# A third stacked-v buffer, a wider gate on the third pair's inputs, and another order of steps in a kernel that chains a gated recurrence into a cosine MLP

## The chip, the cores and the metric

The kernel runs on one core of a Trainium2 chip. The metric is the device time of one execution in microseconds (us). Before the change three runs took 188.55, 185.67 and 186.45 us, a median of 186.45.

## What is computed

The reference is a recurrence over 768 tokens for 4 batches and 8 heads of width 48, and an MLP with the gate h·cos(h) over the 3072 tokens that come out of it:

```python
for t in range(S):
    state = alpha[:, :, t, :, None] * state + np.einsum('bhd,bhe->bhde', k[:, :, t], v[:, :, t])
    y[:, :, t] = np.einsum('bhd,bhde->bhe', q[:, :, t], state)
...
h = x @ w_in            # 384 -> 2048
g = h * np.cos(h)
return (g @ w_out)      # 2048 -> 384
```

All inputs and the output are float32.

## The kernel before

**Tiling.** The tokens of a batch are cut into 3 pieces of 256, so there are 12 pieces J = 0 to 11, which the change calls pairs (each is a pair of chunks c = 0, 1 of 128 tokens; inside a chunk even and odd tokens, e = 0, 1, lie in separate halves). "The third pair" is J = 2, "the fourth" J = 3. Each pair passes the same steps. I write a step as name(J, ...):

- load(J, a/k/q/v): one 384 KB DMA each, issued from SP (L107 to 121). w1(u) and w2(u): a quarter of w_in or w_out each, cast to bf16 on the way, issued from POOL (L125 to 135).
- mula(J) on POOL and ln(J) on ACT make the logarithms of alpha; cums0, cums on PE sum them (L173 to 195); sub, icp, exps (together "eb" for later pairs, L223) make the exponentials; sk(J, e) and sq(J, e) scale k and q with them on POOL or, with ":D", on DVE (L231 to 237); castv(J) on POOL makes the bf16 v (L239).
- trans (PE, L281) and evT (L291) give k and q transposed; scores (PE, L297) and mask (DVE, L306) give the masked products; outer (PE, L313), add (DVE, L330) and state (POOL, L340) carry the state on.
- **Stacked v.** yT needs v with its halves rearranged, in one of NS tiles "vs" (L85), used in turn: vs_t[J % NS]. For J = 0 to 2 this is done by vpe on PE and vev on ACT or DVE (L251 to 261); for later pairs by vst, four SBUF-to-SBUF DMAs of 64 KB from SP (L242 to 247). A vst or vev for pair J must wait until yT(J - NS) has read the tile.
- yT (PE, L347) makes the recurrence's output, evy (L375) copies it as the MLP's input xT.
- m1(J, u) (PE, L385): a quarter of the first matmul, 12 instructions; sin(J, u) on ACT (L393), gate(J, u) on DVE (L398); m2(J, c, part) (PE, L408): 4 instructions; evo copies the result (L422), out writes it (L434, from SP).

The outputs of cums0, vpe, trans, scores, outer, yT and m1 share three PSUM buffers of one tag ("h", two banks each). A step that takes one waits until the last reader of the tile that was there is done.

**What sets the order.** Nothing is scheduled by the compiler. The table PLAN gives every step a number; all steps are issued in the order of these numbers, and each engine (PE, ACT, DVE, POOL, and SP for DMAs) works through its own in that order. An engine that must wait holds everything behind it. IDLE places matmuls on zeros in PE's order, whose results nobody reads.

**A gate.** GATES says that load(2, a) carries a semaphore wait on the last matmul of yT(1). As SP works in order, all loads that come after it in the PLAN wait too.

```python
NL, NQ, NV, NS = 4, 3, 3, 2
...
GATES, AFTER = {("a", 2): ("yT", 1)}, {}
```

Of the kernel before, what the change touches and what calls it, by code (L numbers as in the profile page):

```python
# [16 lines left out]
def kernel(  # L17
# [10 lines left out]
    nc = tc.nc  # L28
    B, H, S, D = q.shape
    DM, DF = moe_w_in.shape  # L30
    C = 128
# [9 lines left out]
    NU = NF // FW  # L41
    MP = 4

    NL, NQ, NV, NS = 4, 3, 3, 2
    BUF = {"a": 4, "in": 3, "cp": 3, "qkT": 3, "A": 2, "un": 4, "us": 2, "c": 3, "xT": 3, "g": 4}

    consts = ctx.enter_context(tc.tile_pool(name="consts", bufs=1))
# [48 lines left out]

    a_sb, kqv, cp_sb, icp_sb, qkT_sb, A_sb, c2_sb = {}, {}, {}, {}, {}, {}, {}
    xT, gsb = {}, {}
    GATES, AFTER = {("a", 2): ("yT", 1)}, {}
    src = {"a": alpha, "k": k, "q": q, "v": v}  # L100

    def pass_gate(step, last):
# [1 line left out]
            if gate == step:  # L104
                AFTER[key] = last

    def load(nm, J):  # L107
        b, g = J // NJB, J % NJB
        t = sb.tile([C, H, 2, D], FP, tag=nm, name=nm, bufs=BUF["a" if nm == "a" else "in"])
        dma = nc.sync.dma_start(  # L110
            out=t.rearrange("p h e d -> p h (e d)"),
            in_=src[nm][b, :, g * T2 : (g + 1) * T2, :].rearrange("h (p e) d -> p h (e d)", e=2),
        )
        if (nm, J) in AFTER:
            tc.add_manual_dep(dma.ins, AFTER[nm, J].ins.name,
                              mybir.DependencyInfo(mybir.DependencyClass.Sync, mybir.DependencyReason.DATA),
                              reason="inputs of later pairs stay behind the weights")
        if nm == "a":
            a_sb[J] = t
        else:  # L120
            kqv[nm, J] = t
# [261 lines left out]
    h_ps, c_sb, o_ps, o_sb = {}, {}, {}, {}  # L383

    def mlp1(J, u):  # L385
        h_ps[J, u] = ps.tile([C, FW, T2], FP, tag="h", name="h_ps", bufs=3)
        for f in range(FW):
            ft = u * FW + f
            for kk in range(KT):
                nc.tensor.matmul(h_ps[J, u][:, f, :], w1[:, kk, ft * C : (ft + 1) * C], xT[J][:, kk, :],  # L390
                                 start=(kk == 0), stop=(kk == KT - 1))

    def cosine(J, u):  # L393
        act_set("trig")
# [13 lines left out]
    def mlp2(J, c, part):  # L408
# [7 lines left out]
        fts = range(part * NF // MP, (part + 1) * NF // MP)  # L416
        for o, cols in zip(o_ps[J, c], HALVES if last_tile else [slice(0, DM)]):
            for ft in fts:
                nc.tensor.matmul(o[:, 0 : cols.stop - cols.start], gsb[J][:, ft, c * C : (c + 1) * C], w2[:, ft, cols],  # L419
                                 start=(done == 1 and ft == fts[0]), stop=(done == MP and ft == fts[-1]))  # L420

    def evict_o(J, c, copy):  # L422
        if (J, c) == (NJ - 1, 1):
# [17 lines left out]
    def idle(n):  # L441
# [3 lines left out]
            nc.tensor.matmul(idle_ps[0], zeros[:, 0:C], zeros, start=True, stop=True)  # L445

    copies = {"DVE": nc.vector.tensor_copy, "ACT": nc.scalar.copy}
    mults = {"DVE": nc.vector, "POOL": nc.gpsimd}
    steps = {
        "load": lambda J, nm: load(nm, J), "w1": load_w1, "w2": load_w2,  # L450
        "mula": mul_a, "ln": ln, "cums0": cums0, "cums": cums, "sub": sub, "icp": icp, "exps": exps, "eb": session,
        "sk": lambda J, e, eng="POOL": scale_k(J, e, mults[eng]), "sq": lambda J, e, eng="POOL": scale_q(J, e, mults[eng]),
        "castv": cast_v, "vst": stack_v, "vpe": stack_v_pe,
# [6 lines left out]


    PLAN = {
# [64 lines left out]
    }  # L527
    IDLE = [(45, 10), (155, 2), (345, 9), (375, 1), (435, 4), (485, 3)]

    order = []  # L530
    for key, line in PLAN.items():
# [42 lines left out]
```

## Time and profile before

| | |
|---|---|
| median of three runs | 186.45 us (185.67 to 188.55) |
| the profiled execution | 185.78 us, of which the span from first to last instruction is 184.0 us |
| busy: PE, DVE, ACT, POOL | 173.0, 134.5, 124.9, 83.5 us |
| first m1 begins | 17.32 us |
| yT(1) begins | 24.28 us |
| first m2 begins | 32.40 us |
| trans(2) begins | 41.26 us |
| last matmul group begins | 179.35 us |

How to read it: the profile is of one execution. Engines' busy times overlap, so the share of PE (94%) says how little of the span it stands still, not how much of its peak it reaches. A DMA's time "to landing" counts from its issue to the moment when its data may be used. A row of the timeline or of the chain of waits gives start, duration, engine, source line, what it writes and reads, and how many instructions were merged; in brackets is the idle time before it and what ended it.

### The profile page before, as it was taken

The numbers are of one execution on the slowest core, as the hardware profiler recorded it, in microseconds if no ns is written. First come the engines' busy times: TensorE is split into PE (matmuls) and PEld (weight loads), VectorE is DVE, ScalarE is ACT, GpSimd is POOL, SyncE is SP. The second block draws the span as 40 slices with busy tenths as digits, with TensorE's granted clock in tenths as the row PEclk, the third lists the DMA queues.
The fourth block names the chain that finished last, engine by engine and source line by source line (L and its number), as shares of the span: only waits on it lengthen the run. The fifth ranks groups of instructions, "written<-read, shape, count | busy, mean of one in ns | idle before, by whom it ended". The sixth has DMA issues, their size and how long they took to land.

```text
span 184.0 us, 5742 instructions
## 1 busy us (share of the span) xinstructions
PE 173.0 (94%) x2457; PEld 125.5 (68%) x2458; DVE 134.5 (73%) x182; ACT 124.9 (68%) x157; POOL 83.5 (45%) x116
## 2 busy tenths in 40 slices
PE   7989579979999999999999999999899999999993
PEld 2445458646687776876787777876687677776672
DVE  7069777669999899799969898879587674734520
ACT  3745457789879999895978989869774517435201
POOL 5388550079883484939686093903901110000000
PEclk9999999999999999999999999999999999999999
DMA  6999999999999979963996579003420121010312
GB/s 146 261 248 224 216 202 206 262 256 257 261 213 262 304 170 278 260 164 85 278 289 154 140 215 245 18 6 88 143 71 4 41 88 51 0 43 4 127 44 86
DMA packets 60137, 29.47 MB, mean 160 GB/s; under 512 B 51024, under 2 KB 60112, under 8 KB 60112
## 3 DMA queue, kind: packets, MB, share of 16 engines
q1 hardware_dynamic: 56256, 25.86, 57.9%
q0 software_dynamic: 3712, 3.15, 10.6%
q8 instruction: 19, 0.31, 0.8%
q10 hardware_dynamic: 144, 0.10, 0.2%
q14 instruction: 6, 0.05, 0.1%
HBM read 25.17 MB, written 4.72 MB: 162 GB/s over the span
## 4 chain that ended last, share of the span: by engine, by line
PE 68%; DMA 11%; issue 7%; SPq 6%; POOL 5%; ACT 1%; DVE 1%; POOLq 0%; DVEq 0%
PE h_ps L390 28%; PE o_ps L419 26%; DMA v<-in_v_dram 6%; SPq L110 4%; PE y_ps L370 4%; DMA k<-in_k_dram 4%; PE A_ps L303 2%; PE T_ps L288 2%; PE U_ps L321 2%; SPq L246 2%; PE o_last L419 1%; DMA vs<-vp 1%; POOL un L343 1%; POOL a L154 1%; PE cums L168 1%
## 5 line engine op out<-in xcount | busy, mean ns | idle before, releaser
L401 DVE TENSOR_TENSOR gsb<-h_ps,c_sb 128x1024 bf16<-128x1024 f32 x48 | 58.4, 1222 | 20.0 <-ACT c_sb L396 18.8
L396 ACT ACTIVATE c_sb<-h_ps,halfpi 128x1024 bf16<-128x1024 f32 x48 | 53.4, 1114 | 28.5 <-PE h_ps L390 28.4
L390 PE MATMUL h_ps<-xT,w 128*128 128x256 bf16 x576 | 67.5, 273 | 0.7 <-DMA w<-in_moe_w_in_dram 0.5
L419 PE MATMUL o_ps<-w,gsb 128*128 128x384 bf16 x368 | 66.7, 326 | 0.0
L390 PEld LDWEIGHTS <-w 128*128 128x128 bf16 x576 | 55.4, 98 | 9.7 <-DMA w<-in_moe_w_in_dram 0.8
L419 PEld LDWEIGHTS <-gsb 128*128 128x128 bf16 x400 | 37.0, 98 | 20.8
L343 POOL TENSOR_TENSOR un<-us,c 128x384 bf16<-128x384 f32 x20 | 16.7, 836 | 33.1 <-DVE us L335 26.0
L309 DVE TENSOR_TENSOR A_sb<-A_ps,msk 128x1024 bf16<-128x1024 f32 x24 | 29.1, 1220 | 3.6 <-PE A_ps L303 3.4
L233 POOL TENSOR_TENSOR kh<-k,icp 128x384 bf16<-128x384 f32 x19 | 19.5, 1032 | 10.2 <-ACT lna L146 5.3
L237 POOL TENSOR_TENSOR qh<-q,cp 128x384 bf16<-128x384 f32 x19 | 18.8, 999 | 6.1 <-ACT cp L219 4.2
L154 POOL TENSOR_TENSOR a<-a 128x384 f32<-128x384 f32 x9 | 9.0, 997 | 11.8 <-DMA a<-in_alpha_dram 11.8
L240 POOL CAST vp<-v 128x768 bf16<-128x768 f32 x12 | 10.1, 853 | 6.4 <-DMA v<-in_v_dram 6.0
L146 ACT ACTIVATE lna<-a 128x768 bf16<-128x768 f32 x12 | 10.1, 842 | 4.1 <-DMA a<-in_alpha_dram 2.4
L141 ACT ACT_TABLE_LOAD x9 | 11.5, 1283 | 0.9 <-PEq L558 0.7
L294 DVE COPY qkT<-T_ps 128x1024 bf16<-128x1024 bf16 x17 | 11.4, 682 | 0.8 <-PE T_ps L288 0.8
L396 ACT ACT_TABLE_LOAD x9 | 11.5, 1283 | 0.2
L431 ACT COPY o_sb<-o_ps 128x384 f32<-128x384 f32 x10 | 4.8, 478 | 9.6 <-PE o_ps L419 9.6
L431 DVE COPY o_sb<-o_ps 128x384 f32<-128x384 f32 x13 | 7.2, 554 | 4.3 <-PE o_ps L419 4.2
L445 PE MATMUL idle_ps<-zeros 128*128 128x512 bf16 x28 | 9.0, 469 | 1.2 <-DVE halfpi L77 1.2
L379 DVE CAST xT<-y_ps 128x384 bf16<-128x384 f32 x14 | 7.7, 584 | 3.1 <-PE y_ps L370 2.9
L335 DVE TENSOR_TENSOR us<-U_ps,un 128x384 f32<-128x384 f32 x16 | 8.8, 551 | 1.3 <-PE U_ps L321 1.2
L303 PE MATMUL A_ps<-qkT 48*128 48x128 bf16 x192 | 8.7, 217 | 0.6 <-DVE qkT L294 0.5
(68 smaller groups left out, 149.2 us busy)
## 6 DMA issues: line engine op xcount, KB each, us to landing
a<-in_alpha_dram SPq DMA_DIRECT2D x12, 384.0 KB, 6.0
v<-in_v_dram SPq DMA_DIRECT2D x12, 384.0 KB, 6.1
k<-in_k_dram SPq DMA_DIRECT2D x12, 384.0 KB, 6.0
q<-in_q_dram SPq DMA_DIRECT2D x12, 384.0 KB, 6.2
out_dram<-o_sb SPq DMA_DIRECT2D x23, 192.0 KB, 2.3
vs<-vp SPq DMA_DIRECT2D x36, 64.0 KB, 2.8
w<-in_moe_w_in_dram POOLq DMA_DIRECT2D x4, 384.0 KB, 8.7
w<-in_moe_w_out_dram POOLq DMA_DIRECT2D x4, 384.0 KB, 10.7
```

Of the source, the lines that this page charges most:

```text
L141: nc.scalar.preload_act_table_set("natural_log_exp_and_others")
L233: eng.tensor_tensor(out=kh_t[J % NQ][:, e, :, 0:D], in0=kqv["k", J][:, :, e], in1=icp_, op=ALU.mult)
L237: eng.tensor_tensor(out=qh_t[J % NQ][:, e, :, 0:D], in0=kqv["q", J][:, :, e], in1=cp, op=ALU.mult)
L294: ins = copy(out=qkT_sb[J][:, c], in_=T_ps[J][:, c].rearrange("r n e s -> r n (e s)"))
L303: last = nc.tensor.matmul(A_ps[J, c][:, a, p, :], qkT[r, c, NP + p, :], qkT[r, c, p, :], start=True, stop=True)
L309: nc.vector.tensor_tensor(out=A_sb[J][:, c].rearrange("s a p t -> s (a p) t"), in0=A_ps.pop((J, c)).rearrange("s a p t -> s (a p) t"), in1 ...
L343: nc.gpsimd.tensor_tensor(out=u, in0=U_sum.pop(n), in1=c2_sb[J][:, :, c].unsqueeze(3).to_broadcast([C, NP, 2, D]), op=ALU.mult)
L390: nc.tensor.matmul(h_ps[J, u][:, f, :], w1[:, kk, ft * C : (ft + 1) * C], xT[J][:, kk, :], start=(kk == 0), stop=(kk == KT - 1))
L396: nc.scalar.activation(out=c_sb[J, u], in_=h_ps[J, u], func=AF.Sin, bias=halfpi, scale=1.0)
L401: nc.vector.tensor_tensor(out=gsb[J][:, u * FW : (u + 1) * FW], in0=h_ps.pop((J, u)), in1=c_sb.pop((J, u)), op=ALU.mult)
L419: nc.tensor.matmul(o[:, 0 : cols.stop - cols.start], gsb[J][:, ft, c * C : (c + 1) * C], w2[:, ft, cols], start=(done == 1 and ft == fts[0 ...
L431: copy(out=t, in_=o_ps.pop((J, c))[0][:, 0:DM])
```

## The change

- NS becomes 3: three tiles vs, so vst(J) and vev(J) wait for yT(J - 3). One more memset on POOL at the start.
- GATES also holds back k, q and v of pair 2 until yT(1). (Before, q of pair 2 was among the first nine loads.)
- load(3, a) stands among the first nine loads and has no gate.
- PLAN and IDLE are other numbers throughout: 31 idle matmuls instead of 28.
- load takes its queue as an argument, which is SP wherever the PLAN names none, and it names none. mlp1 and mlp2 report their last matmul to pass_gate; no gate refers to them.

```diff
-    NL, NQ, NV, NS = 4, 3, 3, 2
+    NL, NQ, NV, NS = 4, 3, 3, 3
...
-    GATES, AFTER = {("a", 2): ("yT", 1)}, {}
+    GATES, AFTER = {("a", 2): ("yT", 1), ("k", 2): ("yT", 1), ("q", 2): ("yT", 1), ("v", 2): ("yT", 1)}, {}
...
-    def load(nm, J):
+    def load(nm, J, queue):
...
-        dma = nc.sync.dma_start(
+        dma = queue.dma_start(
...
-        "load a": "10 20 960 1030 1170 1450 1460 2230 2570 2290 3490 2960",
-        "load k": "70 190 1040 1270 1530 2020 1990 3050 3500 4180 3440 4290",
-        "load q": "100 230 300 1290 1620 1950 2580 2850 3980 4010 3970 4770",
-        "load v": "40 290 1130 1220 1730 1930 1940 3090 3680 2990 4970 4850",
-        "w1": "330 200 470 460 - - - - - - - -",
-        "w2": "260 580 820 690 - - - - - - - -",
+        "load a": "10 100 830 610 1260 1620 1880 2240 2590 2480 3600 3710",
+        "load k": "130 430 1110 1400 1810 2210 2270 2950 3370 2990 3790 4380",
+        "load q": "220 450 870 1430 1820 2000 1980 3210 3540 4160 4510 5270",
+        "load v": "50 400 1140 1500 2140 2920 2260 3690 3570 3810 4860 5240",
+        "w1": "240 210 270 250 - - - - - - - -",
+        "w2": "790 640 860 1070 - - - - - - - -",
...
-        "castv": "90 610 1210 1260 2120 2750 2720 3760 3730 4980 5000 5360",
-        "vst": "- - - 1820 2320 3120 3110 4040 4450 5160 5010 5380",
+        "castv": "110 410 1290 1660 2150 3160 2670 3940 3590 4750 5090 5520",
+        "vst": "- - - 1930 2350 3260 3100 3950 4700 4770 5640 5720",
...
-        "yT": "490 780 1750 2150 2790 3570 3620 4330 4870 5170 5670 5970",
+        "yT": "500 820 1700 2180 2760 3510 3580 4260 4810 5110 5760 5730",
...
-    IDLE = [(45, 10), (155, 2), (345, 9), (375, 1), (435, 4), (485, 3)]
+    IDLE = [(25, 10), (145, 8), (185, 1), (325, 3), (355, 3), (415, 1), (495, 1), (575, 3), (625, 1)]
```

What the numbers mean for the first part of each queue, read from the two PLANs:

```
SP before    a0 a1 v0 k0 q0 k1 q1 v1 q2 | a2 a3 k2 v2 a4 v3 k3 q3 ...
SP after     a0 v0 a1 k0 q0 v1 k1 q1 a3 | a2 q2 k2 v2 a4 k3 q3 out(0,0) v3 ...      (| = the gate on yT(1))
POOL before  castv0 decay0 w1(1) sk(0,1) w2(0) sk(1,1) sk(1,0) w1(0) state(0,0) w1(3) w1(2) w2(1) castv1
             state(0,1) w2(3) decay1 state(1,0) w2(2) state(1,1) mula3 ...
POOL after   castv0 sk(0,0) w1(1) w1(0) w1(3) w1(2) decay0 state(0,0) castv1 sk(1,0) sk(1,1) sq(1,0) decay1
             w2(1) state(0,1) state(1,0) state(1,1) w2(0) w2(2) mula3 w2(3) ...
PE before    ... trans0 outer0 scores0 scores0 vpe0 yT0 trans1 m1(0,1) scores1 vpe1 scores1 outer1 m1(0,0) yT1
             m1(0,3) m1(0,2) m1(1,1) m1(1,2) m1(1,0) m2(0,0,1) m1(1,3) m2(0,0,3) m2(0,0,0) m2(0,0,2) cums02 ...
PE after     ... outer0 trans0 scores0 vpe1 scores0 yT0 trans1 scores1 outer1 scores1 m1(0,1) m1(0,0) m1(0,3) yT1
             m1(0,2) m1(1,1) m1(1,2) m1(1,0) m2(0,0,2) m2(0,0,0) m1(1,3) m2(0,0,1) cums02 m2(0,0,3) ...
```

DVE after, in the same stretch: sk(0,1), add(0,0), vev0, sq(0,1), sq(0,0), evT(0,1), add(0,1), mask(0,1), mask(0,0), sq(1,1), evT(1,1), mask(1,1), add(1,0), mask(1,0), add(1,1), gate(0,1), gate(0,0), gate(0,3). ACT after: evT(0,0), evy(0,0), evy(0,1), evT(1,0), vev1, sin(0,1), sin(0,0), sin(0,3), evy(1,0), evy(1,1), sin(0,2).

More of the change, by code (lines that the diff above doesn't have):

```diff
@@ L389, in mlp1 @@
             for kk in range(KT):
-                nc.tensor.matmul(h_ps[J, u][:, f, :], w1[:, kk, ft * C : (ft + 1) * C], xT[J][:, kk, :],
+                last = nc.tensor.matmul(h_ps[J, u][:, f, :], w1[:, kk, ft * C : (ft + 1) * C], xT[J][:, kk, :],
                                  start=(kk == 0), stop=(kk == KT - 1))
+        pass_gate(("m1", J, u), last)
     def cosine(J, u):
@@ L418, in mlp2 @@
             for ft in fts:
-                nc.tensor.matmul(o[:, 0 : cols.stop - cols.start], gsb[J][:, ft, c * C : (c + 1) * C], w2[:, ft, cols],
+                last = nc.tensor.matmul(o[:, 0 : cols.stop - cols.start], gsb[J][:, ft, c * C : (c + 1) * C], w2[:, ft, cols],
                                  start=(done == 1 and ft == fts[0]), stop=(done == MP and ft == fts[-1]))
+        pass_gate(("m2", J, c, part), last)
     def evict_o(J, c, copy):
@@ L447 @@
     copies = {"DVE": nc.vector.tensor_copy, "ACT": nc.scalar.copy}
+    queues = {"SP": nc.sync, "POOL": nc.gpsimd}
     mults = {"DVE": nc.vector, "POOL": nc.gpsimd}
     steps = {
-        "load": lambda J, nm: load(nm, J), "w1": load_w1, "w2": load_w2,
+        "load": lambda J, nm, eng="SP": load(nm, J, queues[eng]), "w1": load_w1, "w2": load_w2,
         "mula": mul_a, "ln": ln, "cums0": cums0, "cums": cums, "sub": sub, "icp": icp, "exps": exps, "eb": session,
```

110 rows, old and new, of the table PLAN are left out of this document.

## The prediction

> **What bounds the kernel now.** I read the page first, then busy time by stretches, then PE's waits, then the timelines of SP, POOL and PE with each early DMA's time to landing.
>
> ```profile
> span 184.0 us, 5742 instructions
> PE 173.0 (94%) x2457; PEld 125.5 (68%) x2458; DVE 134.5 (73%) x182; ACT 124.9 (68%) x157; POOL 83.5 (45%) x116
> ...
> DMA  6999999999999979963996579003420121010312
> ```
> ```profile
> 17.30:25.20 7.90, 5.34 (x117) 4.12 (x118) 6.10 (x8) 4.21 (x4) 5.30 (x8) 1.00 1.22 215
> ...
> 41.26:58.90 17.64, 17.35 (x319) 12.66 (x319) 16.63 (x22) 15.32 (x21) 14.38 (x17) 1.00 1.11 248
> 58.90:124.00 65.10, 65.08 (x1074) 49.44 (x1068) 56.49 (x69) 55.83 (x72) 39.59 (x49) 1.00 0.76 187
> 124.00:131.00 7.00, 6.20 (x105) 4.10 (x99) 5.36 (x8) 6.88 (x9) 3.94 (x6) 1.00 0.45 115
> 131.00:181.00 50.00, 49.84 (x548) 37.12 (x545) 28.70 (x31) 21.96 (x25) 5.01 (x6) 1.00 0.15 49
> ```
> The first two numbers of a stretch are its length and PE's busy time. From 41.26 us on PE stands still for 0.29 + 0.02 + 0.80 + 0.16 = 1.27 us in all. So a new order can gain almost nothing there except the 0.80, and can lose anything; the rest of what can move lies ahead of 41.26. The 0.80 is one wait, for stacked v:
>
> ```profile
> PE y_ps L370 <- DMA vs<-vp: 0.8, 1, 0.8
> ```
> The early DMAs, first their issues on SP, then on POOL, then the landings of q(1) and v(1) (issued 7.21 and 8.70), q(2) (10.18), w1(1) (8.55), w2(1) (17.18), w2(2) (23.93):
>
> ```profile
> 7.21 1.45 SPq L110 DMA_DIRECT2D q<-in_q_dram  x1
> 8.70 1.44 SPq L110 DMA_DIRECT2D v<-in_v_dram  x1
> 10.18 1.40 SPq L110 DMA_DIRECT2D q<-in_q_dram  x1
> ...
> 122.99 5.70 SPq L246 DMA_DIRECT2D vs<-vp  x8
> ```
> ```profile
> 8.55 0.93 POOL L126 DMA_DIRECT2D w<-in_moe_w_in_dram  x1
> ...
> 17.18 0.78 POOL L132 DMA_DIRECT2D w<-in_moe_w_out_dram  x1
> ...
> 23.93 0.81 POOL L132 DMA_DIRECT2D w<-in_moe_w_out_dram  x1
> ```
> ```profile
> q<-in_q_dram SPq DMA_DIRECT2D x1, 384.0 KB, 6.2
> ...
> v<-in_v_dram SPq DMA_DIRECT2D x1, 384.0 KB, 10.9
> ...
> q<-in_q_dram SPq DMA_DIRECT2D x1, 384.0 KB, 16.3
> ...
> w<-in_moe_w_in_dram POOLq DMA_DIRECT2D x1, 384.0 KB, 6.7
> ...
> w<-in_moe_w_out_dram POOLq DMA_DIRECT2D x1, 384.0 KB, 11.9
> ...
> w<-in_moe_w_out_dram POOLq DMA_DIRECT2D x1, 384.0 KB, 10.9
> ```
> So q(1) landed at 13.4, v(1) at 19.6, q(2) at 26.5: 1.45 us a load while SP's queue is alone (its issue pace), 6.2 and 6.9 once weights run beside it. w1(1) landed at 15.25 and w2(2), the last of eight, at 34.8: (34.8 - 15.25) / 7 = 2.8 us a weight.
>
> **The change, part by part.** Before, v(1) was the eighth load and the late one; k(1) and q(1) were early. After, the slots hold v(0) second (earlier by a slot), v(1) sixth, k(1) seventh, q(1) eighth. What decides when q(1) lands is when the weights begin. POOL now issues w1 behind sk(0,0), which waits for k(0):
>
> ```profile
> 9.03 0.56 DVE L233 TENSOR_TENSOR kh<-k,icp 128x384 bf16<-128x384 f32 x1 [4.49 <-DMA k<-in_k_dram]
> ```
> k(0) keeps its slot (fourth), so sk(0,0) runs from 9.0 to 10.0 (1.0 us like sq below) and w1(1) is issued at 10.0, 1.45 later than before. Before, the weights caught the eighth load; 1.45 later is one load's transfer, so I let q(1) land at 14.9 and only alpha(3) be caught. Bounds: 14.9, and 19.6 (the eighth slot's landing before); I take the low end because the shift is a whole slot.
>
> Then queues, by these durations (mean ns of one after the comma) and PE pieces:
>
> ```profile
> L401 DVE TENSOR_TENSOR gsb<-h_ps,c_sb 128x1024 bf16<-128x1024 f32 x48 | 58.4, 1222 | 20.0 <-ACT c_sb L396 18.8
> ...
> L396 ACT ACTIVATE c_sb<-h_ps,halfpi 128x1024 bf16<-128x1024 f32 x48 | 53.4, 1114 | 28.5 <-PE h_ps L390 28.4
> ...
> L309 DVE TENSOR_TENSOR A_sb<-A_ps,msk 128x1024 bf16<-128x1024 f32 x24 | 29.1, 1220 | 3.6 <-PE A_ps L303 3.4
> ...
> L237 POOL TENSOR_TENSOR qh<-q,cp 128x384 bf16<-128x384 f32 x19 | 18.8, 999 | 6.1 <-ACT cp L219 4.2 <-DMA q<-in_q_dram 1.3 <-ACT qkT L294 0.5
> ...
> L343 POOL TENSOR_TENSOR un<-us,c 128x384 bf16<-128x384 f32 x20 | 16.7, 836 | 33.1 <-DVE us L335 26.0 <-DVE us L337 7.0
> ...
> L240 POOL CAST vp<-v 128x768 bf16<-128x768 f32 x12 | 10.1, 853 | 6.4 <-DMA v<-in_v_dram 6.0 <-issue 0.4
> ...
> L335 DVE TENSOR_TENSOR us<-U_ps,un 128x384 f32<-128x384 f32 x16 | 8.8, 551 | 1.3 <-PE U_ps L321 1.2
> ...
> L294 ACT COPY qkT<-T_ps 128x1024 bf16<-128x1024 bf16 x7 | 7.0, 1010 | 1.9 <-PE T_ps L288 1.8
> ...
> L379 ACT CAST xT<-y_ps 128x384 bf16<-128x384 f32 x10 | 5.7, 597 | 3.7 <-PE y_ps L370 3.6
> ...
> L260 ACT CAST vs<-vs_ps 128x768 bf16<-128x768 f32 x3 | 2.4, 806 | 2.9 <-PE vs_ps L256 2.9
> ```
> ```profile
> 60.95 1.31 PE h_ps L390 x12
> 62.26 0.65 PE o_ps L419 x4
> ...
> 72.68 0.90 PE y_ps L370 x56
> ```
> 1. POOL: four weight issues of about 0.83 to 13.35, decay0 and state(0,0) to 14.4, castv1 to 15.3, sk(1,0), sk(1,1), sq(1,0) to 18.3. Pair 1's trans ends at about 18.95, set by POOL and by yT0 ahead of it (mask(0,0) ends on DVE at 17.45), not by q(1).
> 2. ACT: evy0 twice from 18.4 (1.2), evT(1,0) to 20.55, vev1 to 21.35. The last scores of pair 1 needs vev1's PSUM buffer: 21.4 to 21.75. All of pair 1's attention now stands ahead of the first m1, so m1(0,1) begins at 21.75, against 17.32 before; but then w1 has landed and m1 can follow m1.
> 3. DVE: mask(1,1) to 21.35, add to 21.95, mask(1,0) to 23.15, add(1,1) to 23.7. m1(0,0) waits for that second mask's buffer: 23.2. m1(0,3) 24.5 to 25.8, yT1 to 26.7. m1(0,2) waits for gate(0,0): 27.0. m1(1,1), m1(1,2) follow; m1(1,0) waits for gate(0,2), 30.9 to 32.2, where m2 begins if its weights are there.
> 4. w2(2), which m2(0,0,2) needs first, is issued behind state(1,1), which waits for add(1,1): 24.6 for state's end, w2(0) to 25.4, w2(2) from 25.4. A weight takes 2.8 beside inputs and, since a load's 1.45 is about a fifth of the 6.9 it takes beside weights, some 2.2 alone (an estimate). The five weights ahead land from 10.0 + 6.7 = 16.7 on, two or three of them beside alpha(3) (caught until 14.9 + 6.9 = 21.8), the rest alone: through at about 26.5, and the DMA runs empty. w2(0) lands at 24.6 + 6.7 = 31.3, as a first weight did, w2(2) 2.2 later, at 33.5: m2 waits 1.3. Ends: no wait, and the 11.9 of the longest landing after 25.4, 37.3; the short queue is nearest to the 6.7.
> 5. From 33.5: three m2 and m1(1,3), 3.3, then three more m2, 1.95, and the short cums: PE is at trans(2) somewhat after 38.8. trans(2) also needs k(2) and q(2). Their gate opens at 26.7 instead of 25.24 (yT1's end, first row below), but alpha(3) no longer stands in between. alpha(2) lands while the weights pause; q(2) runs beside them until w2(3) is in, near 36.5, k(2) 1.45 later, at 38. sq(2,0) and sk(2,0), 1.0 each on POOL, behind the exponentials that start at about 38, end at 40 to 40.5; I take 40.5.
>
> ```profile
> 24.61 0.63 PE L370 MATMUL y_ps<-A_sb,vs 128*32 128x128 bf16 x32
> ...
> 41.26 0.57 PE L288 MATMUL T_ps<-ident_bf,kh 64*128 64x64 bf16 x16
> ```
> trans(2) begins at 40.5 against 41.26, but two m2 groups (1.30) are still owed: 41.8, **0.55 later**.
>
> 6. **Third vs buffer.** Before, eight vst DMAs (5.70) started at 122.99, right behind yT(8), which freed the buffer; after, vst(9) waits for yT(6) and its castv stands long ahead of yT(9): **0.80 gone**. What is late next: vst(11) behind castv(11), whose way from outer(10) is add 0.55, state 0.84, castv 0.85, half of the 5.70 and the landing below, 2.8: 7.9 us. PE has two m1 and six m2 groups in between, 6.5, and seven pieces of attention, each shorter than the 0.90 of a yT; at a third of a us each 8.8 in all. No wait, by about one us.
>
> ```profile
> vs<-vp SPq DMA_DIRECT2D x36, 64.0 KB, 2.8
> ...
> L445 PE MATMUL idle_ps<-zeros 128*128 128x512 bf16 x28 | 9.0, 469 | 1.2 <-DVE halfpi L77 1.2
> ```
> 7. **The rest.** vst and out in SP's order hold the loads behind them, but I find each released several us of PE work ahead of its user. yT(6) needs add(6,1) and mask(6,0) behind three other DVE steps: some 0.3 of wait. I add **0.3** (ends 0 and, with DVE or POOL behind, 4). The three more idle matmuls stand where PE waits for ACT, POOL or DVE anyway; without that cover they cost 0.47 each. POOL makes the extra memset while it waits for v(0).
>
> Sum against the profiled execution: 185.78 + 0.55 - 0.80 + 0.3 = 185.8. The median of the runs stands 0.67 above that execution, so 186.5: no change.
>
> **Rivals.** *The weights are in time.* The DMA is empty after 26.5, so w2(0) need not take 6.7. Without the wait of 1.3: 186.5 - 1.3 = 185.2, and 184.9 without the 0.3. Against it: no weight landed sooner than 6.7 before. The Trainium skill ("DMA: Bandwidth & Descriptors", Anatomy of one DMA) has a fit for such DMAs of about 2 us plus the bytes over 436 GB/s; for 768 KB read that is an estimate of 3.8 us, by which w2(2) would be there by about 30 and this rival's time, 185.2, would come. The trace's 6.7 speaks against the rule while queues are shared.
>
> *The weights are late: slower.* Place: m2(0,0,2). w2(2) takes the 10.9 or 11.9 of before and lands at 36.3 to 37.3: 2.8 to 3.8 more, 189.3 to 190.3. From a landing of 11.8 us after issue on it is over 2%. For it: those two rows, and pair 2's loads start right beside it. Against: those two had four weights queued ahead, this one has one or none.
>
> *The weights catch q(1).* It lands at about 18.5, sq(1,0) ends at 19.5, all of steps 2 to 4 move by about 1.0: 187.5.
>
> *The third buffer does nothing*, because castv(9) or SP is late instead: 0.8 back, 187.3; the row of eight vst behind yT(8) speaks against it.
>
> **How the numbers follow.** A measurement of this kernel can tell about 2% (182.7 to 190.2) from no change. My forecast (186.5, with the dead third buffer as its upper edge) has 0.42, weights in time 0.14, q(1) caught 0.11, weights late 0.18, of which 0.10 over 190.2; waits in the long dense run that no row shows, worth 4 us or more, 0.07; a start faster by over 3.7 us, for which nothing speaks but my bounds, 0.08. Faster 0.08, slower 0.10 + 0.07 = 0.17, within 0.75. The range runs from 184.3 (the weights-in-time case less 0.6 of error) to 190.3.
>
> **What would show it.** m1(0,1) near 21.8, yT1 near 26, m2 near 33.5 after a wait for w_out; a dip of the DMA row between 25 and 30 us; trans(2) near 40.5; no wait for vs near yT(9); PE idle under 1 us after 41. Wrong it is made by a first m2 after 36, by q(1) landing after 18, or by waits of PE for masks, evictions or inputs after 45.

## The result, and the profile after the change

The changed kernel takes 186.40 us (median of 20 runs, 185.64 to 187.26), the kernel before 185.74 (20 runs taken beside them). Four of those 20, near 188 us, ran in a slower state of the chip and are left out of the ratio; one of the three runs known at the time of the prediction was such a run, which lifted their median to 186.45. The ratio is 1.0039, with a 95% interval of 1.0026 to 1.0052: slower by 0.7 us, far inside the 2% that the prediction calls no change.

The page of the changed kernel. Its span is 0.6 us longer. In the sixth of the 40 slices (23 to 28 us) the DMA engines moved 133 GB/s, where they had moved 202. The first row of GB/s is that of the changed kernel, the second that of the kernel before.

```profile
span 184.6 us, 5734 instructions
...
GB/s 146 261 261 210 204 133 202 252 246 288 236 162 268 264 169 294 227 158 119 241 281 235 204 186 4 0 97 139 169 86 91 73 44 89 0 14 32 127 87 85
```
```profile
GB/s 146 261 248 224 216 202 206 262 256 257 261 213 262 304 170 278 260 164 85 278 289 154 140 215 245 18 6 88 143 71 4 41 88 51 0 43 4 127 44 86
```

Busy time by the stretches shown before (length, then PE's busy time; the last figures are DMA share and GB/s):

```profile
32.40:41.26 8.86, 7.18 (x58) 4.52 (x56) 4.95 (x7) 7.04 (x10) 2.12 (x2) 1.00 1.14 247
41.26:58.90 17.64, 17.22 (x275) 12.57 (x276) 16.09 (x21) 15.19 (x22) 13.23 (x16) 1.00 0.99 238
58.90:124.00 65.10, 65.06 (x1069) 49.23 (x1067) 56.54 (x69) 56.56 (x74) 40.61 (x50) 1.00 0.76 179
124.00:131.00 7.00, 7.00 (x140) 5.22 (x137) 5.68 (x8) 5.57 (x8) 2.61 (x4) 1.00 0.64 164
131.00:181.00 50.00, 50.00 (x557) 37.02 (x550) 27.30 (x28) 23.11 (x27) 7.30 (x9) 1.00 0.21 66
```
The 0.80 us that PE stood still between 124 and 131 is gone, and 0.16 more behind it. What is new is in the start. PE's timeline there:

```profile
21.97 4.38 PE L390 MATMUL h_ps<-xT,w 128*128 128x256 bf16 x36 [0.30 <-DVE A_sb L309]
26.28 0.52 PE L370 MATMUL y_ps<-qkT,un 128*32 128x128 bf16 x24
...
33.28 1.46 PE L420 MATMUL o_ps<-w,gsb 128*128 128x384 bf16 x8 [0.36 <-DMA w<-in_moe_w_out_dram]
...
37.62 0.32 PE L168 MATMUL cums_h<-lna,tri 128*128 128x384 bf16 x1 [0.91 <-ACT lna L146]
...
41.55 0.41 PE L288 MATMUL T_ps<-ident_bf,kh 64*128 64x64 bf16 x16 [0.69 <-POOL kh L233]
```
trans(2) begins at 41.55 against 41.26, with two m2 groups (1.30) still owed: 1.59 us later by equal work. Less 0.80 and 0.16 that is 0.63. The last matmul group begins at 179.97 against 179.35, 0.62 later.

The logarithms of alpha(2), which cums needs, are late because ACT waits for that load. ACT's row of ln(2) and ln(3):

```profile
36.72 1.57 ACT L146 ACTIVATE lna<-a 128x768 bf16<-128x768 f32 x2 [1.35 <-DMA a<-in_alpha_dram]
```

### The profile page after: what moved, and what is told of

Its sections match the earlier page's. It is cut to its first block, busy times and chain, and to the rows that moved or that the text cites. A ratio compares the mean times of both kernels' runs of the same rounds, so it can differ in the third digit from the quotient of the medians.

```text
span 184.6 us, 5734 instructions
## 1 busy us (share of the span) xinstructions
PE 173.7 (94%) x2460; PEld 125.8 (68%) x2460; DVE 131.8 (71%) x175; ACT 126.3 (68%) x163; POOL 85.7 (46%) x118
## 3 DMA queue, kind: packets, MB, share of 16 engines
q0 software_dynamic: 3712, 3.15, 10.9%
## 4 chain that ended last, share of the span: by engine, by line
PE 76%; DMA 8%; DVE 5%; POOL 4%; issue 3%; SPq 1%; ACT 1%; DVEq 0%; POOLq 0%
PE o_ps L420 30%; PE h_ps L390 30%; PE y_ps L370 5%; DMA a<-in_alpha_dram 5%; PE A_ps L303 3%; DMA k<-in_k_dram 3%; PE T_ps L288 3%; DVE A_sb L309 3%; PE U_ps L321 2%; POOL kh L233 1%; PE o_last L420 1%; POOL w L126 1%; SPq L110 1%; DVE qh L237 1%; PE cums L168 1%
## 5 line engine op out<-in xcount | busy, mean ns | idle before, releaser
L397 ACT ACTIVATE c_sb<-h_ps,halfpi 128x1024 bf16<-128x1024 f32 x48 | 53.1, 1113 | 24.8 <-PE h_ps L390 24.6
L420 PE MATMUL o_ps<-w,gsb 128*128 128x384 bf16 x368 | 67.4, 327 | 0.4 <-DMA w<-in_moe_w_out_dram 0.4
L420 PEld LDWEIGHTS <-gsb 128*128 128x128 bf16 x400 | 36.7, 98 | 21.4 <-issue 0.7
L233 POOL TENSOR_TENSOR kh<-k,icp 128x384 bf16<-128x384 f32 x21 | 21.6, 1035 | 8.2 <-ACT icp L209 5.9
L379 ACT CAST xT<-y_ps 128x384 bf16<-128x384 f32 x13 | 7.0, 595 | 9.4 <-PE y_ps L370 9.4
L433 DVE COPY o_sb<-o_ps 128x384 f32<-128x384 f32 x9 | 5.0, 554 | 10.4 <-PE o_ps L420 10.4
L433 ACT COPY o_sb<-o_ps 128x384 f32<-128x384 f32 x14 | 6.7, 476 | 8.3 <-PE o_ps L420 8.1
L447 PE MATMUL idle_ps<-zeros 128*128 128x512 bf16 x31 | 10.0, 449 | 1.2 <-DVE halfpi L77 1.2
L303 PE MATMUL A_ps<-qkT 48*128 48x128 bf16 x192 | 9.6, 218 | 0.1
```

The lines of the kernel that those rows point to most:

```text
L233: eng.tensor_tensor(out=kh_t[J % NQ][:, e, :, 0:D], in0=kqv["k", J][:, :, e], in1=icp_, op=ALU.mult)
L303: last = nc.tensor.matmul(A_ps[J, c][:, a, p, :], qkT[r, c, NP + p, :], qkT[r, c, p, :], start=True, stop=True)
L397: nc.scalar.activation(out=c_sb[J, u], in_=h_ps[J, u], func=AF.Sin, bias=halfpi, scale=1.0)
L420: last = nc.tensor.matmul(o[:, 0 : cols.stop - cols.start], gsb[J][:, ft, c * C : (c + 1) * C], w2[:, ft, cols], start=(done == 1 and ft = ...
L433: copy(out=t, in_=o_ps.pop((J, c))[0][:, 0:DM])
```

## The experiments

Each was run beside the kernel before; the ratio is to that kernel, with its 95% interval. The profile of a run is of one of its executions, which can lie off the run's median: e5's took 184.78 us (median 185.35), e9's 185.52 (185.86), e3's 186.59 (186.13). Three waits of PE stand in the start (0.36, 0.91 and 0.69 us), and the time came back from one wait in the middle. Theory A is the one on record in the prediction: the third buffer takes the middle wait away, and late DMAs make the start late. Against it stand that the new order does the first by itself, and that PE's order (all of pair 1's attention ahead of the first m1) makes the start late.

### e1: the changed kernel with two vs tiles

```diff
-    NL, NQ, NV, NS = 4, 3, 3, 3
+    NL, NQ, NV, NS = 4, 3, 3, 2
```


> The changed kernel with two vs tiles again, everything else as changed. Theory A (the prediction's step 6: the third tile removed the 0.80 us wait ahead of yT(9)): the wait comes back and the time rises by about 0.8 us over the changed kernel's 186.4, to 187.2. Theory B (the new order alone removed it: vst(9) is issued 16 us ahead of vst(10), and yT(7) and yT(8) are long done when vst(9) and vst(10) are issued): no change, 186.4, no wait for vs in PE's waits.

Measured: 186.22 us, ratio 1.0022 (0.9991 to 1.0053), no wait for vs. Theory B holds: in the new order the third buffer does nothing that these runs can tell. SP's timeline of e1 shows why: vst(9) (the four at 121.23) is issued alone, and the eight of vst(10) and vst(11) only at 137.20, when yT(8) and yT(9), which free their tiles, have long been through PE (122 and 130 us in the changed kernel).

```profile
121.23 2.39 SPq L246 DMA_DIRECT2D vs<-vp  x4
...
137.20 5.79 SPq L246 DMA_DIRECT2D vs<-vp  x8
```

### e2: the kernel before with three vs tiles

```diff
-    NL, NQ, NV, NS = 4, 3, 3, 2
+    NL, NQ, NV, NS = 4, 3, 3, 3
```


> The kernel before with three vs tiles and nothing else changed. Theory A: castv(9) and castv(10) end on POOL at 119.6 us, so the eight vst DMAs are issued some 3 us sooner than 122.99, the 0.80 us wait of yT(9) is gone, and the time falls by about 0.8 us from 185.7 to 184.9. Rival (SP or castv is late anyway): no change.

Measured: 184.16 us beside 185.27, ratio 0.9925 (0.9900 to 0.9951). It beats both kernels. In the old order the buffer is what holds: the eight vst DMAs start at 118.96 instead of 122.99, and the products with vs in yT(9) follow without a wait. e2's SP, then the two parts of yT(9) on PE, before and in e2:

```profile
118.96 5.99 SPq L246 DMA_DIRECT2D vs<-vp  x8
```
```profile
128.89 0.35 PE L370 MATMUL y_ps<-qkT,un 128*32 128x128 bf16 x12
130.04 0.75 PE L370 MATMUL y_ps<-A_sb,vs 128*32 128x128 bf16 x32 [0.80 <-DMA vs<-vp]
```
```profile
128.28 0.35 PE L370 MATMUL y_ps<-qkT,un 128*32 128x128 bf16 x12
128.46 0.62 PE L370 MATMUL y_ps<-A_sb,vs 128*32 128x128 bf16 x32
```
From one start to the other it is 1.15 us before and 0.18 in e2: 0.97 is gone, not 0.80, as the wait that is named is only the last part of the gap. The rest of the gain, 0.1 us by the medians and 0.4 by the ratio, would lie in the start, where e2's profile is 0.6 us ahead at trans(4), 58.29 against 58.90. Of that, 0.41 is a shorter wait of PE for ln(3) at cums(3), 0.59 us against 1.00. Nothing in the edit explains it; it stays open whether it is more than the difference between two executions.

### e3: the changed kernel, w2 issued early

```diff
-        "w2": "790 640 860 1070 - - - - - - - -",
+        "w2": "642 640 644 646 - - - - - - - -",
```


> The changed kernel with w2(0), w2(2), w2(3) issued on POOL directly behind w2(1), at 20 to 22 us instead of 24.8 to 28. Theory A (what the start lost lies in the DMA's pause at 26 to 28 us and in what lands late behind it): the DMA row has no dip, the waits for w_out (0.36), for ln(2) (0.91) and for kh(2) (0.69) shrink, and the time falls by 0.4 to 1.6 us, to 184.8 to 186.0. Rival (the cost is PE's order, all of pair 1's attention ahead of the first m1): at most the 0.36 goes, 186.0 to 186.4.

Measured: 186.13 us, ratio 1.0040 (1.0016 to 1.0064): the time lies in the rival's range, the waits fit neither. Those for w_out and for ln(2) were gone, as theory A wants, but two others took their place: 1.28 us at the second m1, and 0.69 at trans(2) for DVE's sq(2,1). How the first comes about: four issues in a row hold POOL until 21.9 us, state(0,1) behind them is 2 us late, add(1,0) on DVE needs it, mask(1,0) stands behind add(1,0), and the second m1 needs the mask's PSUM buffer. DVE, then PE, of e3:

```profile
22.80 0.56 DVE L335 TENSOR_TENSOR us<-U_ps,un 128x384 f32<-128x384 f32 x1 [1.06 <-POOL un L343]
23.27 1.21 DVE L309 TENSOR_TENSOR A_sb<-A_ps,msk 128x1024 bf16<-128x1024 f32 x1
```
```profile
21.79 1.47 PE L390 MATMUL h_ps<-xT,w 128*128 128x256 bf16 x12 [0.30 <-DVE A_sb L309]
24.54 2.78 PE L390 MATMUL h_ps<-xT,w 128*128 128x256 bf16 x24 [1.28 <-DVE A_sb L309]
...
42.29 0.38 PE L288 MATMUL T_ps<-ident_bf,qh 64*128 64x64 bf16 x14 [0.69 <-DVE qh L237]
```

### e4: the changed kernel, the gate opened by m1(0,1)

```diff
-    GATES, AFTER = {("a", 2): ("yT", 1), ("k", 2): ("yT", 1), ("q", 2): ("yT", 1), ("v", 2): ("yT", 1)}, {}
+    GATES, AFTER = {("a", 2): ("m1", 0, 1), ("k", 2): ("m1", 0, 1), ("q", 2): ("m1", 0, 1), ("v", 2): ("m1", 0, 1)}, {}
```


> The changed kernel with the gate of pair 2's inputs opened by m1(0,1), at about 23.3 us instead of 27.3. Theory A (alpha(2) and k(2) land late because they are issued late): both land some 2 to 4 us sooner, the waits of 0.91 and 0.69 us go, the time falls by up to 1.6 us to 184.8; against it stands that w_out then shares the DMA sooner and the first m2 may wait more than 0.36. Rival (PE's order is the cost): the first m2's wait grows by what the others shrink, 186.0 to 186.9.

Measured: 187.37 us, ratio 1.0110 (1.0060 to 1.0159), worse than either theory gave. alpha(2) is issued at 23.29, the wait at cums is gone, but the inputs take the DMA from w_out and the first m2 stands 2.0 us:

```profile
PE o_ps L420 <- DMA w<-in_moe_w_out_dram: 2.0, 1, 2.0
```
trans(2) gains nothing for it: it is spread from 41.52 to 43.41 and waits for kh and, 0.7 us, for DVE's sq(2,1). So the gate does protect w_out, as long as w_out is issued late.

### e5: the changed kernel, w2(0) and w2(2) in a gap of POOL

```diff
-        "w2": "790 640 860 1070 - - - - - - - -",
+        "w2": "652 640 654 715 - - - - - - - -",
```


> The changed kernel with w2(0) and w2(2) issued on POOL between state(0,1) and state(1,0), in a gap where POOL waits for add(1,0), and w2(3) ahead of mula3. Nothing else on POOL is delayed, unlike in e3, where state(0,1) came 2 us later and add(1,0) and the second m1 with it. Theory A (w_out and alpha(2) land late because the DMA pauses at 26 to 28 us): no dip, first m2 at 32.9 instead of 33.3, alpha(2) a little over 1 us sooner, trans(2) at about 40.5 instead of 41.5, 185.2 to 185.8. Rival (PE's order is the cost): 186.0 or more.

Measured: 185.35 us, ratio 0.9987 (0.9972 to 1.0002), so some 1.0 us less than the changed kernel by the two ratios, whose intervals lie apart. Theory A holds: that PE's order is all of the cost (186.0 or more) is refuted. The slack time of the DMA, first in the changed kernel, then in e5 (DMA share and GB/s at the end of the rows):

```profile
26.00:28.00 2.00, 1.74 (x65) 1.40 (x63) 1.69 (x2) 1.80 (x4) 1.99 (x3) 1.00 0.73 75
```
```profile
26.00:28.00 2.00, 1.74 (x64) 1.56 (x64) 1.92 (x2) 1.88 (x3) 0.41 (x1) 1.00 1.31 203
```
alpha(2) lands 7.6 us after its issue at 27.04, at 34.6; in the changed kernel it took 9.4 from 27.30, to 36.7. The waits for w_out and for ln(2) are gone, and trans(2) begins 1.6 us sooner. ACT, then PE, of e5:

```profile
35.12 1.58 ACT L146 ACTIVATE lna<-a 128x768 bf16<-128x768 f32 x2
```
```profile
32.49 1.46 PE L420 MATMUL o_ps<-w,gsb 128*128 128x384 bf16 x8
...
39.95 0.41 PE L288 MATMUL T_ps<-ident_bf,kh 64*128 64x64 bf16 x16 [0.69 <-POOL kh L233]
```
Of the 1.6, 1.35 is ACT's wait for alpha(2); the other quarter of a us was there before the first moved issue at 20.40 (ACT's copies of yT(0) begin at 18.30 against 18.57), so it belongs to the execution. From ln(2) to trans(2) it is 4.83 us in both kernels, and the 0.69 for kh is in both: it isn't a price of the late load, but the length of the way over ACT and POOL. And no part of the 1.35 comes from the 0.36 for w_out, which delays PE, not ACT.

39.95 + 1.30 = 41.25: by equal work the start of this execution is the old order's (41.26), though its first m1 is 4.4 us later. But the execution is 0.57 us under e5's median, and by the medians e5 is only 0.1 us below the kernel before (0.2 by the ratio), while the waits of 0.80 and 0.16 are gone in it. So these runs don't exclude that some tenths of the cost come from PE's order.

### e6: e5 with alpha(3) and q(2) exchanged

```diff
-        "load a": "10 100 830 610 ...
+        "load a": "10 100 830 840 ...
-        "load q": "220 450 870 ...
+        "load q": "220 450 610 ...
```


> e5's kernel with q(2) among the first nine loads again and alpha(3) behind alpha(2), as before the change. Theory A (the prediction's step 5: alpha(3) early takes a load from in between alpha(2) and k(2), and frees ACT's ln(3)): ln(3) and with it the exponentials of pair 2 wait for alpha(3), trans(2) comes 0.5 to 1.5 us later than in e5, and the time is as much higher. Rival (the exchange is neutral, one load for another): the same as e5 within 0.3.

Measured: 185.89 us, ratio 1.0024 (1.0013 to 1.0035), 0.7 us above e5 by the ratios, 0.5 by the medians. ACT waits for alpha(3) through mula3, in front of pair 2's exponentials, and trans(2) is 1.3 us later. ACT, then PE, of e6:

```profile
37.25 0.84 ACT L146 ACTIVATE lna<-a 128x768 bf16<-128x768 f32 x1 [1.08 <-POOL a L154]
```
```profile
41.25 0.41 PE L288 MATMUL T_ps<-ident_bf,kh 64*128 64x64 bf16 x16 [1.38 <-POOL kh L233]
```
So that part of the change, the fourth pair's alpha among the first inputs, is a gain by itself here.

### e7: e5 with e4's gate

The edits of e4 and e5 together.

> e5's kernel with the gate of pair 2's inputs opened by m1(0,1) as in e4. Theory A (the gate protects w_out: in e4 the inputs let in 4 us sooner pushed the first m2 back by 1.7 us): w_out is issued sooner here, so the first m2 waits less than e4's 2.0 us but more than e5; 185.6 to 186.6, no better than e5. Rival (with w_out issued sooner the gate only costs): trans(2) sooner than in e5 and 0.3 to 1.0 us less than e5.

Measured: 185.39 us, ratio 0.9986 (0.9968 to 1.0004): as e5. With w_out issued in time the earlier inputs cost it nothing, and they bring nothing, since trans(2), begun at 39.69, now waits 0.69 us for DVE's sq(2,1) ahead of its last part, at 41.20. Neither expectation fits fully; theory A's "no better than e5" does.

### e8: e2 with alpha(3) in q(2)'s place

```diff
-        "load a": "10 20 960 1030 ...
+        "load a": "10 20 960 300 ...
-        "load q": "100 230 300 ...
+        "load q": "100 230 1030 ...
```


> The kernel before with three vs tiles (e2, 184.16) and with alpha(3) among the first nine loads in q(2)'s place, q(2) behind alpha(2). Theory A: mula3 and ln(3) no longer wait for alpha(3) (ACT's 1.1 us, PE's 0.6 us at the cums in e2), while q(2), needed only by sq(2), lands at about 37: 0.3 to 0.8 us less than e2, 183.4 to 183.9, the fastest of all. Rival (q(2) becomes what trans(2) waits for): e2's time or more.

Measured: 184.21 us, ratio 0.9939 (0.9911 to 0.9967): e2's time, the rival. The wait at cums(3) went, and PE's busy time from 32.40 to 41.26 rose to 8.80 of 8.86; but ahead of it PE waited 1.6 us for castv(1) instead of e2's 1.0, since v(1) landed 11.0 us after its issue instead of 10.5. Whether that belongs to the exchange or to this execution isn't settled. What the exchange won is lost again a little later: trans(2) begins 0.32 us sooner than in e2 (40.52 against 40.84), but in front of scores(3) PE waits 0.39 us for ACT's copy of pair 3's transposes, and trans(4) begins at 58.26 against 58.29.

### e9: the changed kernel, the gate on alpha(2) alone

```diff
-    GATES, AFTER = {("a", 2): ("yT", 1), ("k", 2): ("yT", 1), ("q", 2): ("yT", 1), ("v", 2): ("yT", 1)}, {}
+    GATES, AFTER = {("a", 2): ("yT", 1)}, {}
```


> The changed kernel with the gate on alpha(2) alone, as before the change; k, q and v of pair 2 carry no wait of their own. Theory A (SP works in order and all three stand behind alpha(2), so their gates do nothing): the changed kernel's time, a ratio to the kernel before of 1.004 within 0.003. Rival (the extra waits cost SP or shift the loads): a change of more than 0.3%.

Measured: 185.86 us, ratio 1.0020 (1.0003 to 1.0038), which overlaps the changed kernel's 1.0026 to 1.0052. Theory A holds: the gates on k, q and v make no difference that can be told; what holds those loads is SP's order.

The profile of e9 also shows how far two executions of nearly the same program lie apart. w2(0), w2(2) and alpha(2) landed 4.9, 6.1 and 8.8 us after issue, not 6.1, 7.6 and 9.4; the first m2 had no wait, and alpha(2), issued at 27.03, cost ACT 0.75 us instead of 1.35:

```profile
35.86 1.58 ACT L146 ACTIVATE lna<-a 128x768 bf16<-128x768 f32 x2 [0.75 <-DMA a<-in_alpha_dram]
```
```profile
40.69 0.41 PE L288 MATMUL T_ps<-ident_bf,kh 64*128 64x64 bf16 x16 [0.69 <-POOL kh L233]
```
ln(2) begins at 36.72, 35.86 and 35.12 in the changed kernel, e9 and e5, and trans(2) 4.83 us later each time: when alpha(2) lands is what moves the start. The 1.59 us is the loss of one execution; e9's, counted the same way, is 0.73.

## Why the prediction was right, and where it was not

No change was forecast, and 186.5 us; the kernel took 186.4. That the two agree to 0.1 us is luck: 0.67 of the 186.5 came from the high median of three runs. Against its own base the forecast was 0.1 us (185.8 against 185.78), and 0.7 was measured. Two steps were off and partly cancelled.

- **Steps 1 to 3 held.** w1(1) was issued at 10.57 (10.0 forecast), and q(1) landed at 8.80 + 6.3 = 15.1 (14.9): the weights began too late to catch it. m1(0,1) began at 21.97 (21.75), yT1 ended near 27.2 (26.7). The queues, added by hand from durations of the old trace, gave each point within 0.6 us.
- **Step 4, the wait of the first m2, was over-sized.** 1.3 was forecast and 0.36 came, since the two loads landed 6.1 and 7.6 us after issue, where I had 6.7 and 8.1. The slack time of the DMA was there (75 GB/s from 26 to 28 us). By the fit of the Trainium skill ("DMA: Bandwidth & Descriptors", Anatomy of one DMA) such a load takes some 3.8 us, an estimate. The soonest took 6.1 here and 4.9 in e9, but that is no clean test of it: w2(1), issued ahead of it, was under way until 27.05 here and 26.7 in e9. The rival of late weights (10.9 to 11.9) did not come; that of weights in time did in the profiled execution of e9, where the first m2 had no wait. That the first m2 began at 33.28, where 33.5 was forecast, is again two errors: PE was ready for it at 32.92 instead of 32.2, and then waited 0.94 us less.

The landings of q(1), w2(0), w2(2) and alpha(2) in the changed kernel, issued at 8.80, 24.84, 25.6 and 27.30 (the last column is the time from issue to landing):

```profile
q<-in_q_dram SPq DMA_DIRECT2D x1, 384.0 KB, 6.3
...
w<-in_moe_w_out_dram POOLq DMA_DIRECT2D x1, 384.0 KB, 6.1
...
w<-in_moe_w_out_dram POOLq DMA_DIRECT2D x1, 384.0 KB, 7.6
...
a<-in_alpha_dram SPq DMA_DIRECT2D x1, 384.0 KB, 9.4
```

- **Step 5 failed.** "alpha(2) lands while the weights pause" is wrong. By step 4's own times w2(0) and w2(2) were issued, at 24.6 and 25.4, before the gate opened at 26.7, and so it came. alpha(2) was issued at 27.30, but SP's queue moved no packet between then and 31.1; from there on it shared the DMA with w2(2) and w2(3), and it landed at 36.7. ACT waited 1.35 us for it, and through cums (0.91) and the exponentials trans(2) began at 41.55, not 40.5: 1.59 us late by equal work, where 0.55 was forecast. e5 shows the cause: three issues of w2 moved on POOL take the 1.35 away. What the step said of alpha(3) is right (e6).
- **Two more errors in step 5 nearly cancel.** The exponentials began at 38.20 where the step has about 38, but only because of the wait; without it they would have begun at 36.85. And the step gives 2.5 us from there to trans(2), where 3.35 were needed: POOL's sq(2,0) began only after two exponentials, 0.95 us, and sk(2,0) took 1.40 us, not 1.0.

The DMA queues of the changed kernel (q0 is POOL's, q1 SP's; packets, MB, share of the 16 engines), from 27.3 to 31.1 us, where q1 has no row, and then from 33 to 34 us:

```profile
q0 software_dynamic: 903, 0.68, 122.3%
```
```profile
q0 software_dynamic: 172, 0.13, 84.6%
q1 hardware_dynamic: 172, 0.07, 39.3%
```

- **Step 6 was right in its size and wrong in its cause.** The 0.80 went, but in this order two buffers do as well (e1). I had argued that the third buffer removes the wait, and not asked whether the new order needs it. In the old order it does what the step says (e2). The rival "the third buffer does nothing" names the right fact with a wrong reason and price: nothing was late, and no 0.8 us came back.
- **Step 7's 0.3 us of waits in the dense run did not come**: from 58.9 us on PE stands still for 0.04 us, where the kernel before, apart from the 0.80, had 0.18. Had the 0.3 come, the loss would have been some 0.9 us instead of 0.6, so this error hid a part of step 5's.

The net, in the profiled executions: 1.59 lost in the start, 0.96 won back later.

## What to carry to other kernels

Where an engine both computes and issues DMAs, a transfer's place in its order is also a place behind every wait of the steps ahead of it; look for a gap in which the engine waits anyway, and put the issue there, not simply early (e5 against e3). A buffer and an order can remove the same wait: before a gain is put down to one, take it out of the changed kernel and put it alone into the old one. An old trace's durations, added queue by queue, placed steps within 0.6 us here, except where two queues share the DMA: there, write down for each load what is in flight when it is issued. A profile is one execution: before a start is called better or worse by some tenths, look at a second one (e9) and at the run's median.

## What the runs showed of the hardware

Loads from SP moved at 1.45 to 1.5 us each while they were alone (in the changed kernel k(1) landed at 13.6 and q(1) at 15.1); beside weights from POOL they took far longer. alpha(3), issued at 10.28, landed 12.8 us later, 8.0 behind q(1), the load ahead of it, while the weights went on landing 2 to 3 us apart. The queue from POOL gets the larger part of a shared DMA: in the rows above both queues move 172 packets in 1 us, but those of POOL are larger, 0.13 MB in all against 0.07. From 17 to 18 us it is 146 packets against 147, and 0.15 MB against 0.06.

A load on an SP queue that stood idle does not start at once while POOL's weights are under way. The first packet of alpha(2) came 2.0 us after issue in e4 (23.29, 25.27), 3.6 in e5 (27.04, 30.62) and 3.9 in the changed kernel (27.30, 31.17). What sets this is not shown.

In e2 and e8 the granted clock fell in the stretch in which PE waits most, to 0.78 and 0.86, and a group of 12 m1 matmuls took 2.74 us (e2) and 2.23 (e8) instead of 1.49. e2's stretch (the clock is the figure 0.78), and its timeline:

```profile
17.30:25.20 7.90, 6.15 (x80) 4.22 (x84) 6.09 (x8) 3.33 (x4) 5.60 (x8) 0.78 1.23 218
```
```profile
22.18 2.74 PE L390 MATMUL h_ps<-xT,w 128*128 128x256 bf16 x12 [0.16 <-DMA w<-in_moe_w_in_dram]
```
The kernel before has longer waits there (1.45 us for castv(1) against 1.02, and a granted clock of 1.00), so what decides it is not shown. e2's first m2 begins at 32.39, as in the kernel before (32.40): the 1.25 us of that group took the place of waits of the kernel before, 0.53 us at yT(1) for a mask and 0.49 for w_in, and of a lead of 0.44 us that e2 had after castv(1).
